# Attention beside a mixture of 64 experts: which row-sum tiles DMA adds in heads 26 to 30, where the last P tiles lie, and when one late load is issued

## The chip, the cores and the metric

The kernel runs on one core of a Trainium2 chip. The metric is the device time of one execution in microseconds (us). Three executions of the kernel before took 1816.3, 1816.33 and 1817.21 us; the median is 1816.33 us.

## The reference, cut to what matters

The input `x` has 2048 tokens of 1024 numbers, all in float32. Two branches are mixed by a gate. Branch A is multi-head attention with 32 heads of width 32, and this case is about its end:

```python
q, k, v = (x @ wqkv) split into 32 heads of width 32
scores  = q @ k.T * 32 ** -0.5            # 2048 x 2048 for each head
p       = softmax(scores)
a       = concat_heads(p @ v) @ wo        # the output projection
b       = ...                             # 32 router heads, top 1 of 64 experts each, gelu
out     = g * a + (1 - g) * b             # g = sigmoid(x . gate_w)
```

## The kernel before, in words

The program has three stages: projections and router (to about 630 us), attention (to about 1629 us) and the output projection. Everything is issued in a hand-written order; nothing reorders it.

**Attention.** For a head `h`, the scores are computed transposed, in 16 tiles `kt` of 128 keys by 2048 queries. A tile (h, kt) is four matmuls of 512 columns (L1289) into a `ring` of seven PSUM banks. ScalarE (ACT) turns the banks into `P[h, kt] = exp(...)` in SBUF (L1298), 128 x 2048 numbers, 1 MB. TensorE (PE) then multiplies P with V into `o` (L1310). The list `batches` alternates about nine score matmuls with the PV matmuls of two or three tiles. A head takes 31 us.

**Row sums.** The softmax needs the sum over all 16 tiles of P. A tile is summed in one of two ways. VectorE (DVE) adds it into an accumulator `acc` (`presum` and `add`, L1351), in two halves of 128 x 1024; every third head's accumulator is the tile `rb`. Or a DMA from the queue of GpSimd (POOL) adds tile `a` into tile `b` in place (`accumulate`, L1340), and DVE later adds `b` alone (`add_pair`, `merge`). `pairs_of(h)` says which pairs (b, a) a head has: (0, 2), (8, 10), and in some heads (4, 6) too. `pair0` below is the add of tile 0 for its pair (0, 2), `pair1` that of tile 4 for (4, 6). A head with two pairs has 13 adds on DVE, one with three has 12. Before, heads 28 and 29 have three pairs and 26, 27 and 30 have two; head 31 has pairs of its own. The table `todo` fixes when each step is issued, counted in tiles from the head's first:

```python
        for b, a in pairs_of(h):
            at(base + b + 4, accumulate, h, b, a)
            three = len(pairs_of(h)) == 3
            at(base + (14 if three else 16), add_pair, h, 0)
            if three:
                at(base + NT + 2, add_pair, h, 1)
            at(base + NT + 6, merge_odd if h == H - 3 else merge, h)
```

So the DVE order of a head is: adds of the plain tiles as they come, the merge of the head before after tile 6, and `pair0` behind the add of tile 13 (three pairs) or of tile 15 (two pairs). `merge_odd` in head 30 (for head 29) is two adds, not one.

**Places.** P tiles live in at most 13 places, `P0` to `P9` and three borrowed ones (`vhl`, `wo_raw2`, `wo_raw3`); from head 27, tile 11 on there are ten. `p_tile` gives a new tile the place with the smallest `until`: 16 tiles after its writing for a tile `b`, 10 for an `a`, 5 for others. ACT may write a tile only when every reader of the whole tile that lay there before is done.

**The last sums.** Behind the last PV, `wo_mm` multiplies the heads' outputs with Wo (L1569) for token chunk 0, except for the group of the last four heads (kc = 7), whose sums are not known yet. In the meantime `rowsum` (L1323) adds the last head's P over the partitions, `norm_sums` copies the result to `ssb` (L1394) and stores it (`smd<-ssb`), `load_r` brings it back (`rr<-smd`), `norm_r` inverts it (L1413, L1414) and stores it (`rd<-rr`), `load_rb` spreads it (`rb<-rd`), and `split_o` applies it (L1637, L100). These small DMAs go through the queue of SyncE (SP), in which also stand the load of `t3l` (1 MB, half of an operand that is used from 1688 us on), `at` (two loads of 128 KB, for the `av_mm` at L1576) and the output `od<-osb` of the last head. The tiles of the projection (`fin`) lie in the memory of the P tiles, so writing one waits for the last reader of the P tiles beneath it.

Of the kernel before, what the change touches and what calls it, by code (L numbers as in the profile page):

```python
# [11 lines left out]
F32R = mybir.dt.float32r  # L12
# [5 lines left out]
S = 2048  # L18
D = 1024
H = 32  # L20
KC = D // 128
HC = KC // 2
NT = S // 128
# [9 lines left out]
def gated_mha_peer_kernel(ctx, tc, xT, wqkv, wv, wo, wq, k12, ug, v, out):  # L33
# [46 lines left out]
    def dma(dst, src, queue=nc.sync):  # L80
        a, b = (ap.bitcast(F32) if ap.dtype == F32R else ap for ap in (dst, src))
        return queue.dma_start(a, b)
# [803 lines left out]
    def x_place(name, dtype=F32R):  # L886
        return xp.tile([128, KC * 512], dtype, name=name)
# [157 lines left out]
    free = x_place("xh3", F32).rearrange("p (a m) -> p a m", m=512)  # L1045
# [105 lines left out]
    def pairs_of(h):  # L1151
        if h == H - 1:
            return (2, 4), (2, 6)
        if h % 4 and h != H - 3:
            return (0, 2), (8, 10)
        return (0, 2), (4, 6), (8, 10)

# [2 lines left out]
    until = [0] * PLACES[0][0]  # L1160

    def p_tile(h, kt):


        k = h * NT + kt
        n = [places for places, k0 in PLACES if k >= k0][-1]
        i = min((i for i in range(n) if i not in (8, 9) or k < H * NT - 8), key=lambda i: until[i])
        pairs = pairs_of(h)
        until[i] = k + (16 if kt in [b for b, _ in pairs] else 10 if kt in [a for _, a in pairs] else 5)
        pool, name = ((pools["right"], f"P{i}") if i < 4 else (pools["left"], f"P{i}") if i < 8 else  # L1170
                      (wk, f"P{i}") if i < 10 else (keep, ("vhl", "wo_raw2", "wo_raw3")[i - 10]))
        P[h, kt] = pool.tile([128, S], F32, name=name, bufs=1)
        return P[h, kt]

    def first_scores():

        tp.close()
        pools.update(right=Pool("ppr", side="right"))
        K, Q = Z
        pt = p_tile(0, 0)  # L1180
        for qc, i in enumerate((5, 6, 0, 1)):
            ps = ps1.tile([128, 512], F32, name=f"bk{i}")
            c = slice(qc * 512, (qc + 1) * 512)
            nc.tensor.matmul(ps, K[:98, :128], Q[:98, c], start=True, stop=True)
            nc.scalar.activation(pt[:, c], ps, AF.Exp, scale=SCALE)
# [90 lines left out]
    def scores(s0, s1):  # L1276


        n = s1 - s0
        banks = ring_banks(n)  # L1280
        cuts = {c for c in range(1, n + 1) if c == n or (s0 + c) % NQ == 0 or banks[c] == 0}
        cuts |= set(range(1, max(1, n - NB) + 1))
        if n <= 2 * NQ:
            cuts |= {c + 2 for c in range(NQ, n, NQ) if not cuts & {c + 1, c + 3}}
        c0 = 0
        for c, i in enumerate(banks):
            (h, kt), qc = divmod((s0 + c) // NQ, NT), (s0 + c) % NQ
            K, Q = KQ[h % 2]
            on_ring(nc.tensor.matmul(ring[:, i, :], K[:98, kt * 128:(kt + 1) * 128],  # L1289
                                     Q[:98, qc * 512:(qc + 1) * 512], start=True, stop=True), i)  # L1290
            if c + 1 not in cuts:
                continue
            m = c + 1 - c0
            q0 = qc + 1 - m
            if q0 == 0:
                p_tile(h, kt)
            i -= m - 1
            on_ring(nc.scalar.activation(  # L1298
                P[h, kt][:, q0 * 512:(q0 + m) * 512].rearrange("p (a m) -> p a m", a=m),
                ring[:, i:i + m, :], AF.Exp, scale=SCALE), *range(i, i + m))  # L1300
            c0 = c + 1
# [25 lines left out]
    def presum(h, kt):  # L1327
        pairs = pairs_of(h)
        first, second = [t for t in range(NT) if t not in sum(pairs, ())][:2]
        if kt in sum(pairs, ()) or kt == first or (h == H - 1 and kt >= NT - 2):  # L1330
            return
        if kt == second:
            if h > 0:
                ACC[h] = T if h % 3 == 2 else wk.tile([128, S], F32, name="acc")
            add(ACC[h], P[h, first], P[h, kt])
        else:
            add(ACC[h], ACC[h], P[h, kt])
# [4 lines left out]
    def pair(h, i):  # L1342
        return P[h, pairs_of(h)[i][0]]
# [40 lines left out]
    def finish(h):  # L1384
        g, j = divmod(h, 4)
        o = wk.tile([128, 512], F32, name="osb")
        nc.scalar.activation(o, O.pop(h), AF.Copy)
        dma(OD[g][32 * j:32 * j + 32, :].rearrange("d (q s) -> q d s", q=NQ), o)


    def norm_sums(h, ps, heads=1):
        g, j = divmod(h, 4)
        o = wk.tile([128, 512], F32, name="ssb")
        ins = nc.scalar.activation(o, ps, AF.Copy)  # L1394
        for i in range(heads):
            dma(SMD[g][j + i:j + i + 1, :].rearrange("o (q s) -> (o q) s", q=NQ), o[32 // heads * i::32, :])
        return ins


    def load_r(g):  # L1400
        R[g] = wk.tile([128, 128], F32, name="rr", bufs=1)
        if g == G - 1:
            dma(R[g][:, :64], SMD[g].rearrange("j (b m) -> (j b) m", m=64))
        else:
            dma(R[g].rearrange("p (r m) -> p r m", r=2), SED[g][:2].rearrange("r j (b m) -> (j b) r m", m=64),
                nc.gpsimd if g == G - 2 else nc.sync)
# [26 lines left out]
    def load_chunk(n, k0, k1, queue=nc.sync):  # L1433
        load_o(n, k0, k1, queue)
        load_rb(n, k0, k1, queue=queue)
# [92 lines left out]
    s0, v0, k = NQ, 0, 0  # L1528
# [21 lines left out]
    fin = Pool("fin")  # L1550
# [9 lines left out]
    def load_at(n):  # L1560
        AT[n] = fin.tile([128, W], F32R, name="at", bufs=3)
        dma(AT[n], ATD[:, n * W:(n + 1) * W])

    def wo_mm(pa, n, kcs, first, last):
        for kc in kcs:
            wh, wl = (W0[0][:, 0], W0[0][:, 1]) if n == kc == 0 else (woh[kc], wol[kc])
            for a, b, i in ((OH[n], wh, 0), (OH[n], wl, 1), (OL[n], wh, 2)):
                for tt, half in pa:
                    nc.tensor.matmul(pa[tt, half], a[:, kc, tt * 128:(tt + 1) * 128],  # L1569
                                     b[:, half * 512:(half + 1) * 512],  # L1570
                                     start=(first and kc == kcs[0] and i == 0),
                                     stop=(last and kc == kcs[-1] and i == 2))
# [19 lines left out]
    def split_hi(kc):  # L1592
        nc.scalar.activation(woh[kc], raw_wo(kc), AF.Copy)
        if kc < KC - 1:
            o = OC[0][:, kc, :]
            nc.vector.tensor_mul(o, o, RB[0][:, kc, :])
            nc.scalar.activation(OH[0][:, kc, :], o, AF.Copy)

    def split_lo(kc):
        nc.vector.tensor_tensor(out=wol[kc], in0=raw_wo(kc),  # L1600
                                in1=woh[kc].bitcast(F32), op=OP.subtract)
        if kc < KC - 1:
            nc.vector.tensor_tensor(out=OL[0][:, kc, :], in0=OC[0][:, kc, :],
                                    in1=OH[0][:, kc, :].bitcast(F32), op=OP.subtract)
# [3 lines left out]
    def load_t(i, p, part):  # L1608

        src, m = TD[i][p], HC // len(part)  # L1610
        for j, place in enumerate(part):
            dma(place, src[:, m * j:m * j + m, :].rearrange("p k m -> p (k m)"))
        ht.b.setdefault(f"T{i + 1}", {})[p] = [place[:, k * 512:(k + 1) * 512] for place in part for k in range(m)]
# [32 lines left out]

    load_t(2, 1, [fin.tile([128, S], F32R, name="t3l")])
    finish(H - 1)  # L1650
    sm = pso.tile([128, 512], F32, name="o")
    list(rowsum(sm, *(P[H - 1, NT - i] for i in (1, 2)), ACC.pop(H - 1)))
    load_chunk(1, 0, KC - 1, nc.gpsimd)
    for n in range(2):
        load_at(n)
    split_hi(1)
    for kc in range(1, KC - 1):
        split_hi(kc + 1)
        if kc == 1:
            norm_sums(H - 1, sm)  # L1660
            load_r(G - 1)
            pso.close()
        split_lo(kc)
        wo_mm(pa, 0, [kc], False, False)
# [160 lines left out]
```

## Time and profile before

| | |
|---|---|
| three timed runs | 1816.3, 1816.33, 1817.21 us |
| the profiled execution | 1816.48 us, of which the span shown is 1814.7 us |
| PE busy | 1799.9 us, 99% of the span |
| DVE, ACT busy | 1503.8 us (83%), 1217.9 us (67%) |
| the chain that ended last | PE 96%, DMA 2%, ACT 1%, issue 1% |
| mean granted TensorE clock | 0.997 |

The shares are means over stages with different limits. During attention ACT, PE and DVE are all near full. Times below are from the start of the span, and `x4` is a count of instructions merged into a row. A row's bracket gives the idle time before it and what ended that. `PEclk` in a table of windows is the granted share of the TensorE clock.

### The profile page before, as it was taken

The page shows a single profiled execution, that of the slowest core. Times are in us where ns is not written, and L with a number is a line of the kernel's source. Part 1 is how long each engine was busy: PE and PEld are TensorE (multiplying, and loading weights), DVE is VectorE, ACT ScalarE, POOL GpSimd, SP SyncE. Part 2 cuts the span into 40 slices and gives each one's busy share as a digit, 9 for nine tenths or more (in the row PEclk, how much of TensorE's full clock was granted, in tenths as well). Part 3 has the DMA queues.
Part 4 walks back from the last instruction along what each step waited for, and adds up shares of the span by engine and source line. Part 5 has one row for each costly group of instructions (what it writes and reads, how often), then busy time and mean ns, then how long its engine had stood idle before and what let it go on. Part 6 is the DMA issues. An engine that isn't in the chain of part 4 may idle for free.

```text
span 1814.7 us, 27897 instructions
## 1 busy us (share of the span) xinstructions
PE 1799.9 (99%) x10567; PEld 1138.0 (63%) x10567; DVE 1503.8 (83%) x1679; ACT 1217.9 (67%) x1608; POOL 270.8 (15%) x335
## 2 busy tenths in 40 slices
PE   9999999999999999999999999999999999999999
PEld 7777777788888755455545555554555544547887
DVE  7868785368987689999999999999999998984584
ACT  4434421211233499999999999999999999972221
POOL 0222000026401210111111111111111111111000
PEclk9999999999999999999999999999999999999999
DMA  6788888723248688899899998898999989957871
GB/s 239 236 283 256 269 263 305 253 71 106 82 141 274 229 189 180 170 189 196 184 209 186 205 196 190 187 200 171 202 198 194 208 185 205 194 104 217 263 182 58
DMA packets 132145, 356.94 MB, mean 197 GB/s; under 512 B 18452, under 2 KB 58788, under 8 KB 107096
## 3 DMA queue, kind: packets, MB, share of 16 engines
q1 hardware_dynamic: 90328, 190.87, 36.4%
q0 software_dynamic: 21520, 128.34, 34.9%
q10 hardware_dynamic: 20160, 35.92, 6.9%
q8 instruction: 84, 1.38, 0.3%
q14 instruction: 53, 0.43, 0.1%
HBM read 176.25 MB, written 86.09 MB: 145 GB/s over the span
## 4 chain that ended last, share of the span: by engine, by line
PE 96%; DMA 2%; ACT 1%; issue 1%; DVE 0%; SPq 0%; ACTq 0%; DVEq 0%
PE ring L1289 28%; PE o L1310 25%; PE bk L155 13%; PE bk L711 10%; PE pa L155 6%; PE bk L758 5%; PE bk L926 2%; PE bk L311 2%; PE pa L1569 2%; PE bk L491 1%; PE bk L395 1%; PE pa L1576 1%; ACT P L1298 1%; DMA wraw<-in_wqkv 1%; DMA smd<-ssb 1%
## 5 line engine op out<-in xcount | busy, mean ns | idle before, releaser
L1298 ACT ACTIVATE P<-ring 128x512 f32<-128x512 f32 (+3 forms) x990 | 807.9, 939 | 20.9 <-PE ring L1289 9.6
L1351 DVE TENSOR_TENSOR acc<-acc,P 128x1024 f32<-128x1024 f32 x420 | 484.1, 1220 | 22.1 <-ACT P L1298 22.0
L1310 PE MATMUL o<-P,V 128*32 128x512 f32 (+1 forms) x4048 | 416.6, 529 | 0.0
L1289 PE MATMUL ring<-Q,K 98*128 98x512 f32 x1024 | 270.9, 408 | 3.6 <-ACT P L1298 3.6
L1289 PE MATMUL ring<-z,z 98*128 98x512 f32 x1020 | 268.2, 407 | 0.0
L1289 PEld LDWEIGHTS ring<-Q,K 98*128 98x128 f32 x1024 | 183.6, 189 | 122.9 <-ACT P L1298 40.7
L1289 PEld LDWEIGHTS ring<-z,z 98*128 98x128 f32 x1020 | 182.1, 188 | 115.3 <-ACT P L1298 39.9
L1310 PEld LDWEIGHTS o<-P,V 128*32 128x32 f32 x4048 | 111.9, 110 | 221.7 <-issue 202.7
L1351 DVE TENSOR_TENSOR rb<-rb,P 128x1024 f32<-128x1024 f32 (+1 forms) x188 | 217.2, 1220 | 8.4 <-ACT P L1298 8.4
L1340 POOL DMA_DIRECT2D P<-P x59 | 53.6, 909 | 469.5 <-PE o L1310 171.2
L1298 ACT ACTIVATE wo_raw<-ring 128x512 f32<-128x512 f32 (+3 forms) x119 | 105.7, 971 | 1.1 <-PE ring L1289 0.2
L240 ACT ACTIVATE hi<-bk 128x512 fp32r<-128x512 f32 x40 | 23.7, 594 | 115.4 <-PE bk L711 96.6
L711 PE MATMUL bk<-xh,e 128*128 128x512 f32 x384 | 94.2, 394 | 0.0
L711 PE MATMUL bk<-xl,e 128*128 128x512 f32 x384 | 92.2, 389 | 0.0
L711 PEld LDWEIGHTS bk<-xh,e 128*128 128x128 f32 x384 | 71.0, 188 | 22.0 <-issue 3.4
L253 DVE TENSOR_TENSOR lo<-bk,hi 128x512 fp32r<-128x512 f32 x40 | 27.6, 689 | 67.6 <-ACT hi L240 65.5
L711 PEld LDWEIGHTS bk<-xl,e 128*128 128x128 f32 x384 | 72.1, 188 | 15.0
L101 DVE TENSOR_TENSOR e<-wraw,e 128x512 fp32r<-128x512 f32 (+3 forms) x64 | 54.5, 859 | 28.1 <-ACT e L100 27.2
L1298 ACT ACTIVATE vhl<-ring 128x512 f32<-128x512 f32 (+3 forms) x83 | 72.8, 951 | 1.4 <-PE ring L1289 0.9
L100 ACT ACTIVATE e<-wraw 128x512 fp32r<-128x512 f32 (+3 forms) x64 | 44.7, 705 | 38.7 <-DMA wraw<-in_wqkv 22.5
L155 PE MATMUL bk<-xh,e 128*128 128x512 f32 x288 | 68.5, 393 | 0.0
L1351 DVE TENSOR_TENSOR acc<-acc,wo_raw 128x1024 f32<-128x1024 f32 x56 | 65.5, 1219 | 2.3 <-ACT wo_raw L1298 2.3
(311 smaller groups left out, 2446.4 us busy)
## 6 DMA issues: line engine op xcount, KB each, us to landing
P<-P POOLq DMA_DIRECT2D x59, 1024.0 KB, 9.6
wqt<-in_wq SPq DMA_DIRECT2D x26, 1024.0 KB
wraw<-in_wqkv SPq DMA_DIRECT2D x30, 512.0 KB
acc<-acc POOLq DMA_DIRECT2D x20, 512.0 KB, 5.4
qdh<-hi ACTq DMA_DIRECT2D x32, 256.0 KB
qdl<-lo ACTq DMA_DIRECT2D x32, 256.0 KB
kdh<-hi ACTq DMA_DIRECT2D x32, 256.0 KB
kdl<-lo ACTq DMA_DIRECT2D x32, 256.0 KB
```

Source lines behind the costliest of these rows:

```text
L100: nc.scalar.activation(hi, src, AF.Copy)
L101: (on or nc.vector).tensor_tensor(out=lo, in0=src, in1=hi.bitcast(F32), op=OP.subtract)
L155: nc.tensor.matmul(ps, self.a[a][i][:, k, :], self.b[b][j][k], start=(not first and k == 0 and i == j == 0), stop=(k == HC - 1 and i == 1))
L311: nc.tensor.matmul(ps[32 * quad:32 * quad + 32, :], kpad[:, quad % 2, i, :], t[:, quad, :], start=(i == 0), stop=(i == 3))
L711: nc.tensor.matmul(ps, t[:, kc // HC, a, kc % HC], x_at(b, n, kc), start=first, stop=last)
L758: nc.tensor.matmul(ps, x_at(a, t // 4, kc)[:, tok], b, start=first, stop=last)
L926: nc.tensor.matmul(p, x_at(a, t // 4, kc)[:, tok], b, start=first, stop=last)
L1289: on_ring(nc.tensor.matmul(ring[:, i, :], K[:98, kt * 128:(kt + 1) * 128], Q[:98, qc * 512:(qc + 1) * 512], start=True, stop=True), i)
L1298: on_ring(nc.scalar.activation(P[h, kt][:, q0 * 512:(q0 + m) * 512].rearrange("p (a m) -> p a m", a=m), ring[:, i:i + m, :], AF.Exp, scale ...
L1310: nc.tensor.matmul(O[h][32 * qc:32 * qc + 32, c0:c1], Vt[g][:, kt, 32 * j:32 * j + 32], p[:, qc * 512 + c0:qc * 512 + c1], start=(kt == 0) ...
L1340: nc.gpsimd.dma_start(P[h, b], P[h, a], accum_op=OP.add)
L1351: nc.vector.tensor_add(out[:, c], a[:, c], b[:, c])
```

## The change

Three edits. Heads 26, 27 and 30 take three pairs in place of two, as heads 28 and 29 do already. The last six tiles of P choose among fewer places: tiles 10 to 13 of head 31 do not take places 0, 3 and 7, and tiles 14 and 15 take one of these. And the loads of `t3l` and `at` move behind the store and the load of the last sums.

```diff
     def pairs_of(h):
         if h == H - 1:
             return (2, 4), (2, 6)
-        if h % 4 and h != H - 3:
+        if h % 4 and h < 26:
             return (0, 2), (8, 10)
         return (0, 2), (4, 6), (8, 10)
...
-        i = min((i for i in range(n) if i not in (8, 9) or k < H * NT - 8), key=lambda i: until[i])
+        free = [i for i in range(n) if i not in (8, 9) or k < H * NT - 8]
+        if k >= H * NT - 6:
+            free = [i for i in free if (i in (0, 3, 7)) == (k >= H * NT - 2)]
+        i = min(free, key=lambda i: until[i])
...
-    load_t(2, 1, [fin.tile([128, S], F32R, name="t3l")])
+    t3l = fin.tile([128, S], F32R, name="t3l")
     finish(H - 1)
...
     load_chunk(1, 0, KC - 1, nc.gpsimd)
-    for n in range(2):
-        load_at(n)
     split_hi(1)
     for kc in range(1, KC - 1):
         split_hi(kc + 1)
         if kc == 1:
             norm_sums(H - 1, sm)
             load_r(G - 1)
+            for n in range(2):
+                load_at(n)
+            load_t(2, 1, [t3l])
             pso.close()
```

The order on DVE in head 30, before: from `merge_odd` of head 29 (the two rows of 64 partitions) to the first add of head 31. `acc_12466` is head 30's accumulator; a tile's name gives its place and a running number.

```order
L1351 TENSOR_TENSOR rb0_5211<-rb0_5211,P5_12278 64x1024 x2
L1351 TENSOR_TENSOR acc_11987<-rb0_5211,P5_12278 64x1024 x2
L1351 TENSOR_TENSOR acc_12466<-acc_12466,P0_12485 128x1024 x2
L1351 TENSOR_TENSOR acc_12466<-acc_12466,P6_12512 128x1024 x2
L1351 TENSOR_TENSOR acc_12466<-acc_12466,P4_12526 128x1024 x2
L1351 TENSOR_TENSOR acc_12466<-acc_12466,P5_12554 128x1024 x2
L1351 TENSOR_TENSOR acc_12466<-acc_12466,P2_12573 128x1024 x2
L1351 TENSOR_TENSOR acc_12466<-acc_12466,P8_12580 128x1024 x2
L1351 TENSOR_TENSOR acc_12466<-acc_12466,P0_12602 128x1024 x2
L1351 TENSOR_TENSOR acc_12466<-acc_12466,P6_12613 128x1024 x2
L1351 TENSOR_TENSOR acc_12466<-acc_12466,P1_12403 128x1024 x2
L1351 TENSOR_TENSOR acc_12679<-P9_12645,P4_12655 128x1024 x2
```

The row next to the last is `pair0`, tile (30, 0) in place P1; eight plain tiles (6, 7, 9, 11 to 15) stand between `merge_odd` and it. The same place now, from the add of tile (30, 5) on; `acc_12464` is head 30's accumulator.

```order
L1354 TENSOR_TENSOR acc_12464<-acc_12464,P9_12472 128x1024 x2
L1354 TENSOR_TENSOR rb0_5211<-rb0_5211,P8_12276 64x1024 x2
L1354 TENSOR_TENSOR acc_11985<-rb0_5211,P8_12276 64x1024 x2
L1354 TENSOR_TENSOR acc_12464<-acc_12464,P3_12506 128x1024 x2
L1354 TENSOR_TENSOR acc_12464<-acc_12464,P1_12520 128x1024 x2
L1354 TENSOR_TENSOR acc_12464<-acc_12464,P8_12549 128x1024 x2
L1354 TENSOR_TENSOR acc_12464<-acc_12464,P9_12568 128x1024 x2
L1354 TENSOR_TENSOR acc_12464<-acc_12464,P3_12575 128x1024 x2
L1354 TENSOR_TENSOR acc_12464<-acc_12464,P0_12401 128x1024 x2
L1354 TENSOR_TENSOR acc_12464<-acc_12464,P7_12597 128x1024 x2
L1354 TENSOR_TENSOR acc_12464<-acc_12464,P1_12608 128x1024 x2
L1354 TENSOR_TENSOR acc_12674<-P0_12642,P2_12652 128x1024 x2
```

`pair0` (tile `P0_12401`) now stands behind five plain tiles (7, 9, 11, 12, 13) and ahead of tiles 14 and 15; tiles 4 and 6 have left this stretch. On ACT, where head 31 begins, before: the last tile of head 30, the copy of a sum, and tiles (31, 0), (31, 1) and the start of (31, 2).

```order
L1298 ACTIVATE P6_12613<-ring_5230 128x2048
L1394 ACTIVATE ssb_12636<-ring_5230 128x512
L1298 ACTIVATE P9_12645<-ring_5230 128x512 x2
L1298 ACTIVATE P9_12645<-ring_5230 128x1024
L1298 ACTIVATE P4_12655<-ring_5230 128x1536
L1298 ACTIVATE P4_12655<-ring_5230 128x512
L1298 ACTIVATE P1_12660<-ring_5230 128x512
```

The same place now.

```order
L1301 ACTIVATE P1_12608<-ring_5230 128x2048
L1397 ACTIVATE ssb_12633<-ring_5230 128x512
L1301 ACTIVATE P0_12642<-ring_5230 128x512 x2
L1301 ACTIVATE P0_12642<-ring_5230 128x1024
L1301 ACTIVATE P2_12652<-ring_5230 128x1536
L1301 ACTIVATE P2_12652<-ring_5230 128x512
L1301 ACTIVATE P8_12657<-ring_5230 128x512
```

Before, it is tile (31, 2) that takes the place P1 of tile (30, 0); now it is tile (31, 0) that takes its place, P0. Tiles (29, 0) and (30, 0) now lie in P0 as well, so in heads 29, 30 and 31 tile 0 takes the place of the tile 0 before it. The queue of SP behind the last PV, before:

```order
L82 DMA t3l<-t2l 128x2048
L82 DMA od_78<-osb 4x32x512
L82 DMA at<-atd 128x256 x2
L82 DMA smd_87<-ssb 4x512
L82 DMA rr<-smd_87 128x64
L82 DMA rd<-rr 128x64
L82 DMA V<-od_78 128x256
```

And now:

```order
L82 DMA od_78<-osb 4x32x512
L82 DMA smd_87<-ssb 4x512
L82 DMA rr<-smd_87 128x64
L82 DMA at<-atd 128x256 x2
L82 DMA t3l<-t2l 128x2048
L82 DMA rd<-rr 128x64
L82 DMA V<-od_78 128x256
```

`t3l` and `at` stood ahead of the sums' store and now stand between the sums' load and the store of their inverses. The memory under `t3l` held places P1 and P2 before, with tile (31, 14) in P2 until its row sum; now tiles 14 and 15 lie in P7 and P0, under `wol4`, `wol5`, `wol7`, `woh0` and `wol0`.

## The prediction

> **What bounds the kernel now.** I first read who PE's matmuls waited for over the whole run. Columns: waiter, releaser, total us, times, longest us.
>
> ```profile
> PE pa L1569 <- ACT z L100: 4.2, 1, 4.2
> PE ring L1289 <- ACT P L1298: 3.6, 2, 3.4
> ```
>
> These are the two largest. PE sets the pace (99% busy), and an edit can bring time only where PE waits or where its clock is low. The table of windows shows that each wait costs more than its idle time. Columns: window, its length, busy us (and instructions) of PE, PEld, DVE, ACT, POOL, granted clock, DMA share, GB/s.
>
> ```profile
> 1562.00:1593.00 31.00, 31.00 (x222) 15.34 (x221) 30.94 (x28) 28.82 (x35) 5.77 (x7) 1.00 0.78 161
> 1597.00:1604.00 7.00, 6.77 (x23) 2.52 (x24) 3.77 (x4) 4.80 (x8) 0.00 (x0) 0.52 0.62 128
> 1657.20:1662.00 4.80, 4.74 (x14) 3.75 (x15) 3.17 (x4) 1.06 (x2) 0.00 (x0) 0.64 0.92 341
> ```
>
> Behind the first wait the clock is 0.52 for 7 us, which costs 7.0 x 0.48 = 3.4 us. Behind the second it is 0.64 for 4.8 us: 4.8 x 0.36 = 1.7 us. The first row also says that DVE is full in head 30 (30.94 of 31 us). The timeline shows the first wait itself.
>
> ```profile
> 1575.61 20.53 DVE L1351 TENSOR_TENSOR acc<-acc,P 128x1024 f32<-128x1024 f32 x18
> 1596.05 2.36 DVE L1351 TENSOR_TENSOR acc<-P,P 128x1024 f32<-128x1024 f32 x2
> 1596.23 0.60 ACT L1298 ACTIVATE P<-ring 128x512 f32<-128x512 f32 x1 [4.50 <-DVE acc L1351]
> 1596.88 0.74 PE L1289 MATMUL ring<-Q,K 98*128 98x512 f32 x1 [3.39 <-ACT P L1298]
> ```
>
> DVE adds without a gap, and the last two of the 18 halves are `pair0` of head 30 (the order in the section on the change). When they end, ACT may write tile (31, 2) into that tile's place, 0.1 us later. Before that, ACT had stood 4.50 us and PE's ring had run full. So a place handed on too late is the cause.
>
> **Heads 26, 27 and 30: what three pairs remove.** A pair takes an add off DVE (two halves; 20.53 / 18 = 1.14 us each, so 2.28 us) and moves `pair0` forward past two more. The same wait stands, smaller, behind the two other changed heads:
>
> ```profile
> 1468.84 3.77 ACT L1298 ACTIVATE P<-ring 128x2048 f32<-128x2048 f32 x4 [0.60 <-DVE rb L1351]
> 1500.45 2.79 ACT L1298 ACTIVATE P<-ring 128x2048 f32<-128x2048 f32 x2 [0.76 <-DVE acc L1351]
> ```
>
> The chain of waits has PE's cost of them: a group of ten score matmuls takes 2.59 us undisturbed, and 3.07 and 3.22 at these two places.
>
> ```profile
> 1439.62 2.59 PE ring L1289 x10
> 1470.58 3.07 PE ring L1289 x10
> 1502.04 3.22 PE ring L1289 x10
> ```
>
> So PE loses 0.48 and 0.63 us, that is ACT's wait less 0.12. With the new places no tile of heads 27 and 28 takes a place less than 2 us after its release (adding 2.28 us per add from the readiness of each tile), so I count both as gone: 1.1 us. For head 31 the wait of 3.6 us and the 3.4 us of low clock go: 7.0 us. ACT itself could be 6.7 us earlier (4.50, and 7.0 - 4.80 = 2.2 us idle in the second window). I take 6.8.
>
> The Trainium skill, "TensorE: Matmul & The Clock Gate", section "Part 1: The HAM clock gate", says that an idle window of about 3.4 us halves the clock and a busy one of that length restores it. By that the low clock behind the first wait would last 3.4 us and cost 1.7, and the forecast would be 1807.3; the row, 7 us at 0.52, does not agree, and it decides.
>
> **What they add: a new place wait at the start of heads 29, 30 and 31.** Tile (h, 0) now takes the place of tile (h-1, 0), which `pair0` releases. Heads 28 and 29 had three pairs already, so their DVE order shows when that is.
>
> ```profile
> 1550.33 13.71 DVE L1351 TENSOR_TENSOR rb<-rb,P 128x1024 f32<-128x1024 f32 x12 [0.40 <-ACT P L1298]
> 1566.30 4.62 DVE L1351 TENSOR_TENSOR acc<-acc,P 128x1024 f32<-128x1024 f32 x4
> 1570.84 2.34 DVE L1351 TENSOR_TENSOR rb<-rb,P 64x1024 f32<-64x1024 f32 x2
> ```
>
> ```profile
> 1555.96 2.02 ACT L1298 ACTIVATE P<-ring 128x512 f32<-128x512 f32 x3
> 1587.90 3.83 ACT L1298 ACTIVATE P<-ring 128x512 f32<-128x512 f32 x5
> ```
>
> The first row starts with tiles 12 and 13 of head 29; its fifth and sixth halves are `pair0`, which ends at 1550.33 + 5 x 1.135 + 1.22 = 1557.2. ACT began tile (30, 0) at 1555.96, so it will stand 1.3 to 1.4 us. This is no backlog: DVE had just waited for ACT (0.40). Head 28 has the same order, so (29, 0) waits as long. For (31, 0): the add of tile (30, 5) was done at 1570.84 at the latest, `merge_odd` takes 4.77 (to 1575.61), then come 7, 9, 11, 12, 13 and `pair0`, 6 x 2.28: 1589.3, against 1587.90, so 1.4 us at most, and 1.0 if the add of tile 5 starts 0.4 us earlier than it could before. At 0.12 less each, PE loses 1.25 + 1.25 + 0.9 to 1.3, up to 3.7 us. If the seven banks of the ring take more of it, since ACT stands only just behind PE at that place, it might be 2.4. I take 3.1. Less than nothing is excluded, since a wait releases nobody earlier. The clock is 1.00 in the windows of the waits that cost 0.48 and 0.63 (rows below) and falls behind 3.39; idle times of 1.2 us are nearer to the first, so I add no low clock. Three falls like the first would be 10 us.
>
> In head 31 DVE has 15 adds behind `pair0`, 34 us, and an estimated 3 us of small work, without a gap: from 1589.3 and a shift of 1.4 (two new waits less 1.1) to 1627.7. PE wants the sum for the last row sum, which takes its last 1 us before 1634.77 (row of `ssb` below), so at 1633.7 - 4.8 = 1628.9. That cover is 1.2 us; beyond it each us of DVE is a us of the total. The added DMA instructions stand in POOL's queue ahead of `fold` and the small row folds, whose readers are a head later.
>
> Attention: 1.1 + 6.8 - 3.1 = 4.8 us earlier.
>
> **The last places and the late load.** The second wait is the way of the last sums. Timeline of SP, ACT, DVE and PE, then the chain:
>
> ```profile
> 1633.97 0.34 SPq L82 DMA_DIRECT2D t3l<-t2l  x1
> ...
> 1635.31 2.01 SPq L82 DMA_DIRECT2D at<-atd  x2
> 1637.43 0.51 SPq L82 DMA_DIRECT2D smd<-ssb  x1
> ...
> 1634.77 0.60 ACT L1394 ACTIVATE ssb<-o 128x512 f32<-128x512 f32 x1 [0.42 <-PE o L1323]
> 1642.73 0.42 DVE L1603 TENSOR_TENSOR acc<-V,z 128x256 fp32r<-128x256 f32 x1
> 1650.66 0.55 DVE L1413 RECIPROCAL rr<-rr 128x64 f32<-128x64 f32 x1 [7.50 <-DMA rr<-smd]
> 1657.26 1.19 PE L1569 MATMUL pa<-woh,z 128*128 128x512 f32 x4 [4.18 <-ACT z L100]
> ```
>
> ```profile
> 1637.43 10.46 DMA smd<-ssb
> 1647.91 2.66 DMA rr<-smd
> ...
> 1651.50 1.44 DMA rd<-rr
> ```
>
> ```profile
> SPq L82 <- PE o L1323: 3.8, 1, 3.8
> ```
>
> SP stood 3.8 us in front of `t3l`, whose memory held tile (31, 14); `od` and `at` stood behind it. The sums were ready at 1635.37, their store was issued at 1637.43 and took 10.46 us for 8 KB, behind 1 + 0.25 + 0.25 MB of `t3l`, `od` and `at` on its own queue. With the edits `od` goes out at once, and `smd` at 1635.4 (all times of this part on the clock of before, without the gain of attention). Its duration lies between 1.44 (`rd`) and 10.46; POOL's loads of chunk 1 are still under way, so I take 4: 1639.4. `rr` lands at 1642.1. DVE is busy with the splits to 1643.15, so the inversion ends at 1644.0, when `rd` goes out (SP has issued `at` and `t3l` by 1642.2). From `rd` to PE it took 1657.26 - 1651.50 = 5.8 us: 1649.8. PE wants this at 1657.26 - 4.18 = 1653.1. So 3.3 us are left for `t3l`, 1 MB that now runs ahead of `rd` and takes 3.2 us at the 325 GB/s of the next 3 us:
>
> ```profile
> 1656.00:1659.00 3.00, 1.74 (x6) 1.41 (x7) 1.99 (x3) 0.58 (x2) 0.00 (x0) 0.90 0.85 325
> ```
>
> The whole wait goes, 4.2 + 1.7 = 5.9 us. `at` is issued by 1642 and read shortly before 1653. The later loads of SP stand behind `rd` and come earlier with it. The new places alone cost nothing: PE has read the tiles under `wol4` and those behind it when DVE gets there.
>
> **Sum.** 4.8 + 5.9 = 10.7 us off the profiled execution's 1816.48 gives 1805.8; the median of the runs is 0.15 lower, so **1805.6 us**.
>
> **Rivals.** A measurement of this kernel can tell about 0.2%, 3.6 us.
>
> *The ring takes the new waits* (10%). Against it: 0.60 and 0.76 us were not taken. 3.1 us more gain: 1802.5.
>
> *The late load delays the inverses instead* (12%). If `smd` is still slow, SP stands at `rr`, and `t3l` is issued only just ahead of `rd`. With 10.46 us from 1635.4, `rd` goes out at 1649.4, and with 3.2 us for `t3l` PE starts at 1658.4, 1 us later than before, at the low clock: 1816.3 - 4.8 + 1.1 = 1812.6; with a part of it 1809. It decides from a landing of `smd` after 1642. The Trainium skill, "DMA: Bandwidth & Descriptors", section "Queues, rings and completion order", speaks for this one: it says that a DMA's semaphore is raised only after every earlier write of that DMA engine, in any queue. By that `smd` waits for POOL's loads and `rd` for all of `t3l`. The 10.46 us agree with it.
>
> *Head starts cost all that head 31 gains* (8%). The three waits add delay in later batches, or the clock falls behind two of them, or DVE becomes the bound in head 31. Attention gains nothing: 1810.4.
>
> *Slower: the added accumulates land too late* (12%). The DMA engines are nearly full where two of the three come:
>
> ```profile
> 1438.00:1469.00 31.00, 31.00 (x220) 15.71 (x216) 29.61 (x26) 30.01 (x40) 5.54 (x7) 1.00 0.99 211
> 1469.00:1500.00 31.00, 31.00 (x216) 15.49 (x212) 29.25 (x26) 30.45 (x38) 4.73 (x6) 1.00 0.87 183
> 1500.00:1531.00 31.00, 31.00 (x216) 15.41 (x208) 26.83 (x27) 30.27 (x37) 4.80 (x6) 1.00 0.90 195
> 1531.00:1562.00 31.00, 31.00 (x218) 15.62 (x217) 27.62 (x25) 30.52 (x39) 4.84 (x6) 1.00 0.99 217
> ```
>
> 1 MB at 211 GB/s is 5.0 us of all engines, so 10 us are added, and 0.25 x 31 = 7.8 us are free. Tile (h, 6) is released by the landing, and in heads 29, 30 and 31 tile (h+1, 1) takes its place. In head 30 the accumulate follows the first of these, a row of POOL; the second, of the DMA table, is the same accumulate in head 28, with us to landing at the end:
>
> ```profile
> 1575.87 0.81 POOL L1363 DMA_DIRECT2D acc<-rb  x1 [4.35 <-DVE acc L1351]
> ```
>
> ```profile
> P<-P POOLq DMA_DIRECT2D x1, 1024.0 KB, 9.6
> ```
>
> It is issued at about 1576.5, and (31, 1) begins 1.9 us after 1587.90, so it decides from a landing time of 13 us; now it is 9.6. At 18 us ACT stands 5 us at each of three heads, and PE 4.9 us and 3.4 us of low clock: 25 - 10.7, so 1830; halfway 1820.
>
> *The waits come back elsewhere* (6%): 1816.
>
> *Forecast* (52%): 1805.6, with its own range 1803 to 1808.
>
> **Numbers.** The range 1801.5 to 1812.6 takes in the free ring, the bounds of the new waits, the tail and the third rival; outside are the last two cases, 18%. Faster by over 0.2%: 52 + 10 + 12 + 8 = 82%. Same: 6%. Slower: 12%.
>
> **What would show it.** Right: ACT stands 1.0 to 1.4 us at the first tile of heads 29, 30 and 31, released by DVE; no wait behind heads 26 and 27; no low clock in head 31; `smd` issued right behind `ssb` and landing in under 7 us; no wait of PE before the last group of chunk 0. Wrong: an ACT wait released by a DMA, a wait of PE of 3 us anywhere in attention, or `rd` landing over 3 us after its issue.

## The result and the profile after

The changed kernel takes 1809.05 us (median of six runs, 1807.22 to 1811.72), the kernel before 1816.14 beside it: ratio 0.9962, 95% interval 0.9949 to 0.9975, so 7.1 us (0.4%) faster. Forecast were 10.7 us; the profiled execution (1810.25 us) shows 6.2.

PE's waits of the changed kernel (waiter, releaser, total us, times, longest us):

```profile
PE pa L1572 <- ACT z L100: 2.9, 1, 2.9
PE ring L1292 <- ACT P L1301: 1.8, 3, 0.7
```

The wait of 3.4 us in front of head 31 is gone; three small ones stand elsewhere. The wait in the tail has shrunk from 4.2 to 2.9 us instead of going. The table of windows at the start of head 31 and behind the tail's wait (window, length, busy us of PE, PEld, DVE, ACT, POOL, granted clock, DMA share, GB/s) shows no low clock any more:

```profile
1590.00:1600.00 10.00, 10.00 (x63) 4.96 (x62) 10.00 (x10) 9.51 (x15) 0.77 (x1) 1.00 0.61 122
1651.00:1656.00 5.00, 4.54 (x20) 3.74 (x21) 3.17 (x4) 1.47 (x2) 0.00 (x0) 1.00 0.91 339
```

ACT's timeline at the starts of heads 29, 30 and 31, with the accumulate of head 28 (POOL) ahead:

```profile
1510.91 1.20 POOL L1343 DMA_DIRECT2D P<-P  x1
...
1524.73 2.07 ACT L1301 ACTIVATE P<-ring 128x512 f32<-128x512 f32 x4 [1.31 <-PE ring L1292]
1527.88 2.37 ACT L1301 ACTIVATE P<-ring 128x2048 f32<-128x2048 f32 x2 [1.08 <-DMA P<-P]
1558.24 4.26 ACT L1301 ACTIVATE P<-ring 128x512 f32<-128x512 f32 x5 [1.24 <-DVE rb L1354]
1590.65 4.33 ACT L1301 ACTIVATE P<-ring 128x512 f32<-128x512 f32 x6 [0.49 <-PE ring L1292]
```

Rows two, four and five are the forecast place waits at tiles (29, 0), (30, 0) and (31, 0). In rows two and five the profile names the ring; the tile's place came free 0.1 us before the start there too. Row three was not forecast: tile (29, 1) stands 1.08 us until an accumulate issued 17 us earlier has landed. The tail, from the chain of waits:

```profile
1630.88 6.80 DMA smd<-ssb
1637.70 3.24 DMA rr<-smd
...
1641.80 5.07 DMA rd<-rr
```

And from SP's timeline:

```profile
1639.46 0.62 SPq L82 DMA_DIRECT2D t3l<-t2l  x1
1641.80 0.32 SPq L82 DMA_DIRECT2D rd<-rr  x1
```

`smd` goes out right behind the sums and lands in 6.80 us instead of 10.46. But `rd`, 1.44 us before, takes 5.07 with `t3l` issued 2.3 us ahead of it on the same queue.

PE runs the same 10567 matmuls in the same order in every kernel here, so the start of one matmul can be compared across traces. The table gives, for one profiled execution of each kernel, how much earlier (minus) than before the stretch makes the next matmul start: *attention* from head 26 (1436.0 on the clock of before) to the first projection behind the PV products (1628.9), *tail* from there to 1665.1, *behind* from there to the end. What a run is ahead or behind by at 1436 (up to 0.8 us) is in none of them. The ratio is to the kernel before in the same set of runs; beside e8 to e10 one of its nine runs, 2529.5 us at a granted clock of 0.654, is left out.

| kernel | median us (range) | ratio, 95% interval | attention | tail | behind |
|---|---|---|---|---|---|
| after | 1809.05 (1807.2–1811.7) | 0.9962 (0.9949–0.9975) | −4.0 | −2.9 | +1.1 |
| after, again (a2) | 1811.28 (1807.5–1815.3) | 0.9961 (0.9947–0.9974) | −0.5 | −0.1 | 0.0 |
| e1 pairs alone | 1807.69 (1805.7–1810.6) | 0.9946 (0.9933–0.9960) | −2.1 | −5.7 | 0.0 |
| e2 load move alone | 1812.78 (1810.5–1816.4) | 0.9977 (0.9967–0.9988) | −0.9 | −4.3 | +0.5 |
| e3 after, `t3l` first | 1806.73 (1805.8–1810.4) | 0.9947 (0.9933–0.9960) | −4.8 | −5.8 | +0.1 |
| e4 after, other places | 1807.87 (1805.8–1810.6) | 0.9945 (0.9931–0.9958) | −7.0 | +0.8 | 0.0 |
| e5 = e3 + e4 | 1806.63 (1806.0–1811.5) | 0.9949 (0.9935–0.9963) | −8.3 | −3.1 | 0.0 |
| e6 pair in head 30, load move | 1805.10 (1804.2–1807.7) | 0.9934 (0.9921–0.9948) | −7.2 | −3.8 | 0.0 |
| e7 chunk 1's loads late | 1818.57 (1817.3–1819.9) | 1.0005 (0.9996–1.0014) | −1.9 | +6.0 | −0.1 |
| e8 after, `t3l` behind `rd` | 1808.84 (1808.2–1810.8) | 0.9959 (0.9945–0.9973) | −5.2 | −5.4 | +2.9 |
| e9 = e4 + e8 | 1807.18 (1805.8–1808.7) | 0.9949 (0.9934–0.9963) | −8.4 | −5.8 | +2.7 |
| e10 = e6 + e8's `t3l` | 1804.83 (1804.1–1808.8) | 0.9938 (0.9924–0.9952) | −7.2 | −6.1 | +4.6 |
| e11 pair in head 30, `at` late | **1804.11** (1802.8–1804.7) | 0.9925 (0.9912–0.9939) | −7.2 | −5.8 | +0.7 |

### The profile page after: what moved, and what is told of

The parts are those of the page before. It is cut to its first block, busy times and chain, and to the rows that moved or that the text cites. A ratio compares the mean times of both kernels' runs of the same rounds, so it can differ in the third digit from the quotient of the medians.

```text
span 1808.5 us, 27885 instructions
## 1 busy us (share of the span) xinstructions
PE 1795.6 (99%) x10567; PEld 1134.8 (63%) x10567; DVE 1497.6 (83%) x1673; ACT 1218.7 (67%) x1608; POOL 273.8 (15%) x338
## 4 chain that ended last, share of the span: by engine, by line
PE 95%; DMA 3%; ACT 1%; DVE 1%; issue 0%; SPq 0%; ACTq 0%; DVEq 0%
PE ring L1292 28%; PE o L1313 25%; PE bk L155 13%; PE bk L711 10%; PE pa L155 6%; PE bk L758 5%; PE bk L926 2%; PE bk L311 2%; PE pa L1572 2%; PE bk L491 1%; PE bk L395 1%; DMA P<-P 1%; ACT P L1301 1%; PE pa L1579 1%; DMA woh<-t3h 0%; DMA wraw<-in_wqkv 0%
```

## The experiments: the parts alone

**e1, pairs alone:** `pairs_of` as changed; places of the last tiles and the two loads as before.

> The third pair in heads 26, 27 and 30 alone; the last tiles' places and the order of the late loads stay those of before. Theory (the gain is the sum of two separate parts): attention gains about 4 us as in the trace of after (1.1 and 7.2 us of waits removed, 4.4 us of new ones), the tail keeps its PE wait of about 4 us and its low clock: 1816.1 - 4.0 = 1812. Rival (most of the gain comes from the tail, the pairs only shift the wait): 1815 to 1816.

Measured 0.9946: by the medians this part alone gains at least as much as the whole change. The expectation (1812) missed. The tail's wait goes without the two other edits, as SP's timeline and the chain show:

```profile
1623.36 0.34 SPq L82 DMA_DIRECT2D t3l<-t2l  x1
...
1633.01 0.50 SPq L82 DMA_DIRECT2D smd<-ssb  x1
```

```profile
1633.01 7.31 DMA smd<-ssb
...
1643.66 1.44 DMA rd<-rr
```

Other pairs are other places: tiles (31, 14) and (31, 15) no longer lie under `t3l`, so its load goes out 3.3 us ahead of the end of the PV products (1626.66 in the chain), not 5 us behind it as before. It is down before the sums come, and `rd` has its 1.44 us back. What attention loses against e3 starts at tile (29, 1): ACT stands 1.91 us there, until 17.8 us behind the issue of the accumulate that holds the tile's place (the profile names PE).

**e2, the load move alone:**

```diff
-    load_t(2, 1, [fin.tile([128, S], F32R, name="t3l")])
+    t3l = fin.tile([128, S], F32R, name="t3l")
...
-    for n in range(2):
-        load_at(n)
...
             load_r(G - 1)
+            for n in range(2):
+                load_at(n)
+            load_t(2, 1, [t3l])
```

> The move of the loads of at and t3l behind the last sums alone; pairs and places as before. Theory: attention keeps the PE wait of 3.4 us in front of head 31 and its low clock; smd lands about 7 us after its issue and rd about 5, as after the change, so the tail gains about 3 us: 1816.1 - 3.0 = 1813. Rival (the tail's gain needs the new places or the earlier end of attention): within 1 us of 1816.

Measured 1812.78 us (0.9977, 4.3 us), as expected. PE's wait, then the chain:

```profile
PE pa L1569 <- ACT z L100: 1.5, 1, 1.5
```

```profile
1634.49 6.81 DMA smd<-ssb
...
1644.14 4.88 DMA rd<-rr
```

The two durations are those of the changed kernel within 0.2 us, with other pairs and other places, so neither the pairs nor the places are needed for them. A wait of 1.5 us stays, 2.9 in the changed kernel. The table's −0.9 for attention, in which this run changes nothing, shows what a single profile can differ by behind a low clock: the wait in front of head 31 is the same 3.4 us, but the clock in the window 1600 to 1604 is 0.77 against 0.53 before.

## The experiments: the tail

**e3, `t3l` first again** (after, with `t3l`'s load ahead of `od`; `at` stays behind the sums).

> The changed kernel with the load of t3l put back to its first position, ahead of od; at stays behind the sums, and the new places let t3l go out without a wait on the row sum. Theory A (rd lands in 5.07 us because t3l stands ahead of it on its queue): rd lands in 1.5 to 2 us, smd still in about 7, the PE wait of 2.9 us ahead of the last group of chunk 0 goes or falls under 0.5: 2 to 3 us under the changed kernel, 1806 to 1807. Rival B (t3l, wherever it stands, meets the small transfers): smd takes 9 to 10 us again because t3l is now ahead of it, the PE wait stays at 2 us or more: 1809 or more.

```profile
1620.94 0.34 SPq L82 DMA_DIRECT2D t3l<-t2l  x1
...
1631.37 0.50 SPq L82 DMA_DIRECT2D smd<-ssb  x1
1637.19 0.33 SPq L82 DMA_DIRECT2D rr<-smd  x1
...
1642.09 0.32 SPq L82 DMA_DIRECT2D rd<-rr  x1
...
1643.59 2.54 SPq L82 DMA_DIRECT2D rb<-rd  x4
```

`rd` is followed by its reader 1.5 us later, `smd` takes 5.82, and PE waits nowhere in the tail: −5.8 us. Theory A holds, and the time of 1806.73 was expected; the ratio is that of e1.

**e7, the loads of chunk 1 late:** e3 with `load_chunk(1, 0, KC - 1, nc.gpsimd)` taken out and `load_chunk(1, 0, KC - 1)` put behind `norm_r(G - 1)`, so on SP's queue.

> The load of t3l first, and the loads of chunk 1 (od and rd, 14 transfers on POOL's queue) moved to SP's queue, behind rd of chunk 0's inverses. Theory A (smd takes 5.8 to 7.3 us instead of the 1.4 of rd because the loads of chunk 1 run beside it): smd lands in 1.5 to 3 us and DVE, no longer a DMA, is the last thing ahead of the inversion; no PE wait ahead of the last group, but none was there to remove: the time stays at 1805 to 1808 unless SP's longer queue makes chunk 1 late. Rival B (a small transfer from one partition row takes 6 us in any case): smd stays at 6 us or more.

(The timeline shows 11 transfers, not 14.) SP's timeline:

```profile
1633.01 0.50 SPq L82 DMA_DIRECT2D smd<-ssb  x1
1634.69 0.33 SPq L82 DMA_DIRECT2D rr<-smd  x1
```

`smd` lands in 1.68 us, against 5.82 in e3, from which this run differs by the loads of chunk 1 alone. So some 4 us of e3's landing are these loads beside it: theory A. The kernel gains nothing by it, because chunk 0's `rb` now stands behind those loads on SP's queue and PE waits 10.3 us: 1818.57. The Trainium skill, "DMA: Bandwidth & Descriptors", section "Queues, rings and completion order", says that a completion is written only behind all earlier writes of the same DMA engine in any of its queues. The traces agree: 1.68 us here, 5.06 to 11.27 behind or beside megabytes.

**e8, `t3l` behind `rd`** (after, with `load_t(2, 1, [t3l])` moved behind the loop that loads the last pieces of chunks 0 and 1 and `t0`).

> The changed kernel with one edit: the load of t3l goes out not ahead of rd but behind it, behind the last pieces of chunk 0 and 1 and of t0l (its reader on PE comes at about 1680). Theory A (of the 5.9 us of the tail, those not gained are t3l's: rd or rr lands with it): rr in 2 to 3 us, rd in about 1.5, smd as before that in 6 to 7, and the PE wait ahead of the last group of chunk 0 under 0.6: 2.5 to 3 us under the changed kernel, whose attention stays as it is: 1806 to 1809. Rival B (the loads of chunk 1 alone make the sums late): the PE wait stays at 1.5 us or more.

The tail gains 5.4 us, `rd` takes 1.44 and PE waits 0.3 us, but the time is that of the changed kernel. (`rr` took 5.34 us against an expected 2 to 3, with no `t3l` issued yet, so `t3l` is not all that makes it late.) Half of the tail's gain is given back 45 us later: the chain, and the timelines of SP (`t3l` and the third `at`), DVE and PE.

```profile
1685.53 8.02 DMA woh<-t3h
```

```profile
1649.19 0.36 SPq L82 DMA_DIRECT2D t3l<-t2l  x1
...
1665.22 2.61 SPq L82 DMA_DIRECT2D at<-atd  x1
...
1692.42 2.36 DVE L1625 TENSOR_TENSOR V<-V,P 128x1024 f32<-128x1024 f32 x2 [7.59 <-DMA P<-rd]
...
1694.41 0.50 PE L155 MATMUL pa<-woh,acc 128*128 128x512 f32 x1 [1.91 <-ACT acc L100]
```

A load of this queue is the last thing ahead of DVE's scaling, ACT's rounding and PE's matmul: chunk 3's `P<-rd` by the timeline, `woh<-t3h` right behind it by the chain. SP issues load upon load from the inverses to there, and 1 MB more in that stretch makes everything behind it later: `at` goes out at 1665.22, against 1659.95 in e11, where `t3l` went out ahead of the sums. PE in e11 is 2.5 us ahead at that point, so 2.8 of the 5.3 us are the queue's. So theory A holds for the tail; of the time, 1808.84, it holds only the upper end (1806 to 1809), and the 2.5 to 3 us under the changed kernel are not there.

## The experiments: the places

**e4, other places in heads 26 to 30:**

```diff
+        if k >= 26 * NT and h < H - 1 and kt in (0, 6):
+            until[i] += 2
```

> The changed kernel, but tiles 0 and 6 of heads 26 to 30 count as two tiles longer in use, so that tile (h+1, 0) and (h+1, 1) do not take the places that are freed last. Theory A (the new place waits at the starts of heads 29, 30 and 31 cost about 4.4 us together, 1.25 of it for a landing): no ACT wait of over 0.3 us at these starts, no wait for a DMA there, and 3.5 to 4.4 us under the changed kernel: about 1805. Rival C (ACT or DVE, nearly full there, gives it back at the next tile): waits of the same total elsewhere, 1808 to 1809.

Attention gains 7.0 us instead of 4.0, and no tile at the starts of heads 29 to 31 waits for a place. One wait is new, 0.9 us of PE and 1.64 of ACT in head 30:

```profile
1581.66 5.61 ACT L1303 ACTIVATE P<-ring 128x1536 f32<-128x1536 f32 x6 [1.64 <-PE ring L1294]
```

The profile names the ring, but it is a landing again, at another tile: by the rule of `p_tile`, (30, 13) now takes the place of (30, 2), and the accumulate that reads this one was issued at 1567.90 and landed 13.7 us later, 0.1 us ahead of the row. e5 and e9, with the same places, get that landing in time (in e5 by less than 0.2 us) and gain 8.3 and 8.4. So theory A holds at the starts of the heads, and its time of 1805 missed by 3 us: the tail lost what attention gained (PE's wait, then the chain):

```profile
PE pa L1574 <- ACT z L100: 3.9, 1, 3.9
```

```profile
1628.29 7.32 DMA smd<-ssb
...
1638.81 6.73 DMA rd<-rr
```

Here `t3l` went out only 1.3 us ahead of `rd`, `rd` took 6.73, and behind PE's wait the clock was 0.50 from 1649 to 1654.

**e5, both** (e3 + e4).

> The load of t3l first again and, in heads 26 to 30, tiles 0 and 6 counted two tiles longer in use: the two separate parts together. Theory (the place waits cost about 4 us in attention, the late load about 4 us in the tail, and they add): attention ends 2.5 to 3 us ahead of the changed kernel's, the tail has no PE wait: 1803 to 1804, the best of all. Rival (with attention earlier the sums meet more of the loads of chunk 1, so smd lands later and the PE wait returns): 1806 to 1808.

SP's timeline, the chain and PE's wait, and, for comparison, SP's timeline of e9 below, which has the same places but `t3l` behind `rd`:

```profile
1625.05 0.34 SPq L82 DMA_DIRECT2D t3l<-t2l  x1
```

```profile
1627.54 11.27 DMA smd<-ssb
```

```profile
PE pa L1574 <- ACT z L100: 2.7, 1, 2.7
```

```profile
1627.41 0.50 SPq L82 DMA_DIRECT2D smd<-ssb  x1
1633.55 0.34 SPq L82 DMA_DIRECT2D rr<-smd  x1
```

The two do not add. With e4's places `t3l` waits for a later tile and goes out 2.5 us ahead of `smd` instead of 10, and `smd` takes 11.27. The time is the rival's, but its mechanism, that earlier sums meet more of chunk 1's loads, is not what did it: in e9 the sums are as early, and `smd` takes 6.14. It is the late `t3l` ahead of it.

**e6, the third pair in head 30 alone** (e2 with `if h % 4 and h < 28:`).

> Pairs as before except in head 30, which gets the third one; the loads of at and t3l behind the sums, no choice of places for the last tiles. Here tile (31, 0) takes the place of tile (30, 6), which an accumulate releases when it has landed. Theory A (landing takes 16 us or more where the DMA engines are full, as at head 29 of the changed kernel): ACT stands 4 to 5 us at tile (31, 0), released by a DMA, and the gain of head 31 is gone: 1812. Theory B (with heads 26 and 27 at two pairs the engines have room and it lands in 10 to 12 us): no such wait, the 7.2 us of head 31 are gained: 1805.5 to 1806.5.

Theory B, 0.4 us under its range: 1805.10. Tile (31, 0) takes the place that the accumulate of head 30 releases. The accumulate is issued here, lands 10.2 us later, and the tile starts after 12 us without a wait (POOL's and ACT's timelines):

```profile
1576.08 1.21 POOL L1340 DMA_DIRECT2D P<-P  x1
...
1588.51 4.32 ACT L1298 ACTIVATE P<-ring 128x512 f32<-128x512 f32 x6
```

All of head 31's gain is there (−7.2), with two of the three added accumulates left out; the starts of heads 29 and 30 have no wait.

**a2, the changed kernel again**, in one set with e5 to e7.

> The changed kernel itself, once more, beside the others of this call. Theory (its runs spread because the accumulate of head 28 lands sometimes ahead of and sometimes behind the moment at which tile (29, 1) wants its place): 1807 to 1812 again, with the ACT wait at tile (29, 1) anywhere from 0 to 2 us, and the PE wait of about 3 us ahead of the last group of chunk 0. Rival (the spread is that of the chip and shows in the kernel before as much): the two spread alike.

It spread from 1807.49 to 1815.29, the kernel before from 1816.01 to 1819.10. The profiled execution is the longest one. ACT's timeline, the chain, and two rows of the table of windows:

```profile
1561.66 2.37 ACT L1301 ACTIVATE P<-ring 128x2048 f32<-128x2048 f32 x2 [2.69 <-DMA P<-P]
```

```profile
1634.31 5.06 DMA smd<-ssb
1639.38 7.11 DMA rr<-smd
```

```profile
1563.00:1567.00 4.00, 3.36 (x11) 1.54 (x15) 1.03 (x1) 4.00 (x7) 0.00 (x0) 0.79 0.70 179
1654.00:1658.00 4.00, 3.14 (x7) 2.48 (x8) 2.40 (x4) 1.47 (x2) 0.00 (x0) 0.50 0.90 319
```

The theory named the right mechanism and the wrong tile: tile (29, 1) waits for nothing this time, the landing wait stands at tile (30, 1), 2.69 us, with a low clock behind it, and 0.36 us of ACT at tile (31, 1). The spread goes beyond the expected 1812, and the rival does not fit: the kernel before spreads by 3.1 us, this one by 7.8. In the tail it is `rr`, issued 1.8 us ahead of `t3l`, that lands late (7.11); whether `t3l` does it is open, as e8 shows. The PE wait is 2.9 us again, but with a low clock behind it. So the time of the changed kernel hangs on where landings fall beside the moments at which they are wanted, in attention and in the tail.

What makes the accumulates late can be seen on one that every kernel has, tile 6 of head 28 into tile 4. The DMA tables of after and of e6 have it, with us to landing at the end:

```profile
P<-P POOLq DMA_DIRECT2D x1, 1024.0 KB, 16.9
```

```profile
P<-P POOLq DMA_DIRECT2D x1, 1024.0 KB, 9.4
```

It takes 9.4 to 9.6 us in the five profiles with two pairs in heads 26 and 27 (before, e2, e6, e10, e11) and 13.8 to 17.7 in the nine with three, so the accumulates added in heads 26 and 27 make it late. From 1469 to 1500 the DMA share is 0.87 before and 1.04 after.

**e9** (e4 + e8) and **e10** (e6 + e8's `t3l`):

> The same, and in heads 26 to 30 tiles 0 and 6 counted two tiles longer in use. Theory (attention gains 8.3 us without any new place wait, the tail 5.5 to 5.9, and the two add): 1803 to 1804, and the runs spread less than the changed kernel's since no tile waits for a landing. Rival (the sums of the last head, earlier by 8 us, meet all the loads of chunk 1, as where smd took 11.27 us): 1806.

> The pairs of before but for head 30, which gets the third one, no choice of places for the last tiles, and the load of t3l behind rd as in the other two. Theory: attention gains 7.2 us, the waits of 0.6 and 0.75 us behind heads 26 and 27 stay, the PE wait of 1.9 us goes: 1803 to 1804. Rival (the third pairs of heads 26 and 27 are needed for head 31): 1806 or more.

Attention and tail add as expected, −14.2 and −13.2 us up to 1665. Both give back 2.7 and 4.6 us behind it as e8 does. Both times missed, e9's by 3 us (it lies above the rival's, too) and e10's median by 0.8 (its profiled execution, 1808.21, is one of its longer ones). In e9, where no tile waits for a landing, the runs spread by 2.9 us.

**e11**, the kernel before with two edits: `if h % 4 and h < 28:`, and the two `load_at` behind `load_r(G - 1)`; `t3l`'s load stays first.

> The kernel before with two edits: the third pair in head 30 alone, and the loads of at behind the sums; t3l's load stays first, and the places that follow from the pairs put neither of the last two tiles under it. Theory (a full queue in the second unit of outputs takes back what the late t3l gives the first, so its 1 MB has to land ahead of the sums): t3l goes out 3 to 4 us ahead of the end of the PV products, smd lands in 6 to 7 us, no PE wait of over 0.6 us ahead of the last group of chunk 0 and none of over 0.5 us between 1690 and 1705; attention gains 7.2 and the tail 5.5 us: 1803 to 1804.5. Rival (t3l is held by a later tile, as where it went out 4 us behind the end of the products and smd took 11.27 us): 1806.

SP's timeline:

```profile
1620.15 0.34 SPq L82 DMA_DIRECT2D t3l<-t2l  x1
...
1628.11 0.50 SPq L82 DMA_DIRECT2D smd<-ssb  x1
1635.67 0.33 SPq L82 DMA_DIRECT2D rr<-smd  x1
...
1639.22 0.32 SPq L82 DMA_DIRECT2D rd<-rr  x1
...
1659.95 0.79 SPq L82 DMA_DIRECT2D at<-atd  x1
```

1804.11 us, as expected, ratio 0.9925: the lowest of all, with the narrowest range, though its interval overlaps those of e6 and e10. `smd` takes 7.56 us, more than expected, but no PE wait is left in the tail, and 0.7 us is given back behind it. It does without the third pairs in heads 26 and 27, the choice of places and the late `t3l`. That `at` has to move is not shown: e1, which leaves it in front, has the same tail (−5.7).

## Why the prediction was right in direction and some 3.5 us too far

The time lies in the stated range (1801.5 to 1812.6) and 1 us above the forecast's own (1803 to 1808). By terms:

- **Waits behind heads 26 and 27:** 1.1 forecast (0.48 and 0.63). Comparing starts of the same matmuls again, in the nine profiles with these pairs PE is 0.45 to 0.50 us earlier behind the first place (1475 on the clock of before) and 1.12 to 1.18 behind both (1522). Right.
- **Head 31:** 6.8 forecast, 7.2 measured in after, e6, e8 and e11. Right; the low clock went with the wait. e6, e10 and e11, with the third pair in head 30 alone, have all of it.
- **The three place waits:** 3.1 forecast. e8, which has no landing wait, is 1.96 us later at the end of head 30 although the 1.14 us above are gone: 3.1 us (ACT stands 1.29, 1.23 and 0.49). The places are right, and the mechanism. That the sum is right is in part luck: 3.1 was taken between 3.7 and 2.4 for a ring that might take part of it; the ring took none, and the third wait was 0.49, not 1.0 to 1.4.
- **The landing:** the slower rival's mechanism, taken as not acting, acts in some runs. Its point was a landing of 13 us; the accumulates that held tiles took 17 (after) and 19 us (a2) from issue. But its price was set too high: the wait was 0.31 us of ACT in e3, 1.08 in after, 1.50 in e7, 1.91 in e1, 2.69 (and 0.36) in a2 and none in e8, at one head or two and never at three. Against e8, attention lost 1.2 us more in after and 4.7 in a2, the low clock behind it included. That the added accumulates make landings late is shown (a2); that it is the full engines, and not the longer queue, is not. e4 shows that a late landing costs nothing where no tile wants the place yet: head 29's took 16.8 us there.
- **The tail:** 5.9 forecast, 2.9 gained. This is the step that failed: it makes 3.0 of the 4.5 us by which the profiled execution falls short (attention makes 0.8, the stretch behind the tail 1.1, and 0.5 it was ahead before head 26). The wait and its low clock were worth what the prediction said (5.4 to 6.1 us in e1, e3 and e8 to e11); the term of the sum that was mis-sized is the landing of `smd`: 4 us taken, 6.80 measured. The 3.3 us left for `t3l` shrank by that. The smaller terms nearly cancel: `rd` with `t3l` ahead of it 5.07 against 1.44 + 3.2, `rr` 3.24 against 2.66, the way from `rd` to PE 0.2 longer, DVE's inversion 1.0 earlier behind `rr`. 2.8 + 0.4 + 0.6 + 0.2 - 1.0, less the 3.3 - 3.2 = 0.1 to spare, is the 2.9 of the wait that is left; the low clock still went. The second rival's point, `smd` down after 1642 on the clock of before, was just met (1637.70 and the 4.5 us that the run is ahead: 1642.2), and its mechanism came in by half: `t3l` went out 2.3 us ahead of `rd` and delayed it. For a part of this rival the prediction named 1809; that the measured 1809.05 meets it so closely is luck, since the stretch behind the tail was in no sum. That `t3l` ahead of `rd` takes the rest is shown by e3 and e8, and that chunk 1's loads make `smd` late by e7.
- **Behind the tail:** not in the sum at all. The profiled execution gives 1.1 us back between 1695 and 1706 on the clock of before, at chunk 3's load; e8 to e10 show why (2.7 to 4.6 us). The remark that the later loads "come earlier with it" missed that 1 MB more stands among them.
- **"The new places alone cost nothing"** was right of their cost and missed their point: the pairs alone had already moved the tiles from under `t3l` (e1). By the table the two other edits bring nothing on top of the pairs; 0.9946 (e1) and 0.9962 (after) come from two sets of runs and their intervals overlap, so that they cost something is not shown.

Of the marks set out beforehand for right, no wait behind heads 26 and 27, no low clock in head 31, `smd` right behind `ssb` and under 7 us (6.80) were seen; the ACT waits at the first tiles were 1.31, 1.24 and 0.49, the last under its range; and PE did wait before the last group of chunk 0, 2.9 us. Two of the three signs named for wrong appeared: the ACT wait released by a DMA and `rd` over 3 us.

## What to carry to other kernels

Changing which steps use a buffer longer changes which places all later tiles get; list the takers and their releasers for the whole rest of the program, since both a gain (`t3l`'s load freed) and the loss (three place waits, and tiles that wait for a landing in some runs) came by that road. A small transfer on the critical way pays for the megabytes issued just ahead of it or beside it: move the large one to where it lands before, and not to where a later stretch has a full queue. A wait that depends on a landing near the moment of need shows as a wide range of runs (7.8 us in a2, 1.9 in e11); one profile does not give its price.

## What the runs showed of the hardware

Behind 3.39 us (before, head 31), 3.9 (e4) and 4.18 us (before, tail) of idle time of PE the granted clock fell to about half. A shorter idle time lowers it in some runs and not in others. Behind 2.9 us the clock is 1.00 in the changed kernel's first profile and 0.50 in a2's. In e10 it falls behind 1.73 us, as its timeline of PE and table of windows show; in e8 it stays at 1.00 behind 1.91 us, the last row.

```profile
1692.37 0.50 PE L155 MATMUL pa<-woh,acc 128*128 128x512 f32 x1 [1.73 <-ACT acc L100]
...
1694.00:1698.00 4.00, 4.00 (x12) 3.13 (x11) 2.50 (x4) 1.26 (x2) 0.00 (x0) 0.60 1.05 390
```

```profile
1694.00:1698.00 4.00, 3.30 (x13) 2.44 (x14) 3.22 (x5) 0.99 (x2) 0.00 (x0) 1.00 1.05 398
```

So a wait of just under 2 us costs about that or some 3.4 us, by run: the ten matmuls behind it took 4.14 us in e10 and 2.57 in e8, by the chain. The Trainium skill, "TensorE: Matmul & The Clock Gate", section "Part 1: The HAM clock gate", gives an idle window of about 3.4 us, free-running, as what lowers the clock; the fall behind 1.73 us does not agree with a whole idle window, and what else was counted there is open.

The same 8 KB transfer from the sums took between 1.68 us (e7) and 11.27 us (e5), and the same 1 MB accumulate of head 28 between 9.4 and 17.7 us, by what else was under way.
